# A second order for every step and load ahead of the experts, in an attention and mixture-of-experts kernel

## Chip, cores and metric

The kernel runs on one core of a Trainium2 chip. The metric is the device time of one execution in microseconds (us), lower is better. A core has the matrix engine (PE, with its weight loads shown as PEld), the vector engine (DVE), the scalar engine (ACT), GpSimd (POOL) and SP, which here issues all DMA transfers from one queue. [...]

## What is computed

Three blocks follow each other on 1152 tokens (2 batches of 576):

```
scores = q k^T / 8, masked: 4 heads to the last 32 positions, 4 heads to every 4th of the last 128
x  = softmax(scores) v                                # 8 heads of 64 -> 512 columns
h  = x w_in;  s = h softmax(h);  ln = (s - mean) / sqrt(var + 1e-6) * g      # 512 -> 1024
y  = ln w_out                                         # 1024 -> 512
out = sum over 4 experts of p_e relu(y w1_e) w2_e     # 512 -> 1024 -> 512
```

The matrices w_in and w_out come as 64-bit floats and are converted on the chip. Every large product is made of three: a value is split into a high part that the fast product takes exactly and a low part, and high x high, high x low and low x high are added up.

## The kernel before

The program is written out by hand, without a planner at run time: each engine executes its instructions in the order in which the program issues them, and semaphores make one engine wait for another. For everything up to the first half of expert 0 that order is a text, `ORDER`, of 542 entries. An entry is a load (a DMA from SP), a batch of warm-up products or the next step of a generator, and the loop that plays it is short:

```
for name in ORDER.split():
    name, _, n = name.partition("*")
    alt[0] = name.endswith("+")
    ...
        if name not in gens:
            gens[name] = makers[part[0]](*args)
        next(gens[name], None)
```

So the n-th time that `H.3` stands in the text, the n-th step of generator `H.3` is issued, and the text decides for each engine, and for SP's queue, what stands ahead of what. A sign `+` behind a name sets `alt`: in that step `pick()` gives POOL and not DVE, `copy` DVE and not ACT, `poolv` DVE and not POOL. The names:

- `F.n`: n warm-up products of constant data (L86). `lP`, `lD`: loads of a q/k tile (L151), by t and batch. `lvp`, `lvd`: of v (L159, L154). `lI.j`: of a quarter of w_in (L209, L212; `lI.4` and `lI.0` are the two halves of quarter 0). `lO`: of w_out (L228). `misc`: of small constants. `lW`, `lV`: of expert weights (L477).
- `UP.t.b`, `UD.t.b`: an attention unit, windowed or dilated heads: mask and scores (L266, L275), row maximum (L296), difference (L298), exponential (L301), sum (L303), reciprocal (L305), multiply (L307), transpose on PE (L326) and copy, or for five units of batch 1 a transpose on DVE (L312) that goes through DRAM (L316, L320), value product (L337), high part (L176 or L174) and low part (L250).
- `VI.j`, `VO.j.t`: conversion of a piece of w_in or w_out: two steps on ACT (L190, L192), two on DVE (L194, L196), an add (L198, `pick()`), the high part, the low part (L225, `pick()`; for w_out L241).
- `H.t`: the product of token tile t with w_in in four groups of six (L367), the maximum (L372), the exponential (L374), the weighted product (L376) and the scaling (L379 on ACT or L381 on DVE). The first group of `H.0` needs `UP.0.0` and quarter 0 of w_in.
- `T.t`: the transpose of tile t: tiles 0 to 2 on PE (L398), with a high and a low part; tiles 3 to 8 with a transpose on DVE (L412, L414), a write to DRAM (L419, L422), a read-back (L428, L431), the high part (L176 or L174) and the low part (L436, `pick()`).
- `X.c.d`: the product of three tiles with w_out (L449); `X.0` needs tiles 0 to 2, `X.1` 3 to 5, `X.2` 6 to 8. `endA`, `endE`, `endH`, `endX` give memory back; `sc` makes the row scales (L664 to L671).
- `WP`, `WV`, `XQ`: splits and sums of the expert weights and of y for a Strassen product (L481); `u.s`: its seven products for a half of the tokens (L562); `d.t`: the down product (L634).

PSUM has two rings of two tiles: `psa` for attention, the transposes of tiles 0 to 2 and half of the expert products, `psm` for warm-ups, `H`, `X` and the other half. A product waits until the tile before the last one in its ring has been read. Behind `ORDER` loops write out the other seven expert halves in a fixed order.

Of the kernel before, what the change touches and what calls it, by code (L numbers as in the profile page):

```python
# [28 lines left out]
ASWAP = ("UD.0.1", "UD.1.1", "UD.2.1", "UP.1.1", "UP.2.1")  # L29

ORDER = """
F.3 lP.0.0+ UP.0.0 lI.4 VI.4+ lD.0.0 VI.4 F.1 UP.0.0+ UP.0.0 lD.1.0+ VI.4 F.1 lP.1.0+ UD.0.0 UD.1.0 UP.0.0 VI.4 lI.0 UP.0.0+ VI.4 VI.0 lP.2.0 UD.0.0 UD.0.0+
UD.0.0+ UP.1.0 UP.0.0+ VI.4+ UP.0.0+ UD.1.0 UD.1.0+ UP.1.0 F.10 lD.2.0+ UP.2.0 UD.1.0+ VI.0 UD.0.0 VI.0+ VI.0 UP.1.0+ UD.1.0 UP.1.0+ VI.4+ lI.1+ UD.1.0+ VI.0+
UD.2.0+ UD.1.0+ lI.2+ F.3 UD.0.0 UD.0.0+ VI.0 UP.1.0+ UP.2.0 lvp.0.0+ VI.1+ VI.1+ UP.1.0+ UP.2.0+ VI.0 lvd.1.0+ F.1 UP.0.0 UD.2.0 UD.2.0 UP.2.0 UP.0.0 F.4
UD.1.0 UD.0.0 F.3 VI.1+ UD.1.0 VI.2+ UP.0.0 VI.2 UD.0.0 UP.2.0+ UP.1.0+ VI.1 UP.0.0 VI.1 VI.1 VI.2 UP.0.0+ lI.3 UD.1.0+ VI.2+ UP.1.0 lvp.1.0 UD.1.0 H.0+ lvd.0.0
UP.1.0 VI.3 UP.2.0+ UD.1.0+ UP.1.0 UD.2.0 UD.0.0+ VI.1 VI.3+ VI.2 VI.3 UP.1.0 UP.1.0 lD.1.1+ UD.0.0 lO.0.0+ H.0+ UD.1.1 VI.3 VI.2 UD.2.0+ lO.0.1 misc+ UD.1.1
H.1 UD.2.0 lD.0.1+ lvd.2.0+ UP.2.0+ UD.1.1+ UD.0.0 VO.0.1 VI.2+ lvp.0.1 lP.0.1 UD.2.0 lvd.2.1 H.1 VO.0.1+ UD.2.0 UD.2.0 UD.0.1 VI.3 VO.0.1+ UD.1.1 UP.0.1 UD.0.1
VI.3 lD.2.1 lvp.2.0+ lP.2.1 UD.1.1 UP.0.1 H.0 UD.0.1+ UD.0.1 UP.0.1+ UD.0.1+ UD.0.1+ UD.2.0 VO.0.1+ VI.3+ VO.0.0 UD.2.1 VO.0.0 lP.1.1+ VO.0.1+ H.0 lO.1.1+
VO.0.0 UD.2.1+ UD.2.0 UP.0.1+ UD.2.0 UD.0.1+ H.0+ H.1 H.0+ UD.0.1+ UD.0.1 UD.2.1 VO.0.0 H.1 H.0 UD.0.1+ UD.1.1 endE+ VO.0.0+ UD.2.1+ UP.2.0 UP.2.0 UD.1.1+
UP.2.1+ lvd.0.1+ VO.0.1+ lvd.1.1 UP.2.1+ UP.0.1 UD.2.1+ UP.2.0 UP.0.1 UP.2.0 VO.1.1+ VO.0.1+ VO.1.1 H.2 H.2+ H.1+ UP.2.1+ H.0+ UP.0.1+ UD.1.1+ VO.0.0+ UP.0.1  # L40
VO.1.1+ UP.2.0 VO.0.0+ H.1+ T.0 UP.2.1 UP.0.1 T.0+ UD.1.1 UD.2.1+ lO.1.0+ H.1+ T.0 UP.0.1 VO.1.1+ VO.1.1+ H.3+ UP.2.1 lO.2.1+ H.2+ T.0+ VO.1.0+ UP.0.1 UP.0.1+
VO.1.0 UD.1.1 VO.1.1+ UP.2.1+ UP.1.1+ UD.0.1 VO.1.0+ UP.1.1+ VO.1.0 H.2+ VO.1.0+ UP.1.1 UP.2.1+ UD.0.1+ UD.0.1+ H.3+ UD.2.1+ UD.1.1 H.2 H.1+ VO.1.0 UP.1.1+ T.1+
H.3+ lO.2.0+ UD.2.1+ H.2+ UD.1.1 H.3 UD.1.1 UD.2.1+ VO.2.1+ UP.1.1 VO.1.0+ H.4+ VO.2.0 VO.1.1 UP.2.1 VO.2.0 T.1+ T.2 T.1 H.3+ UP.1.1 UP.1.1+ VO.2.0+ H.4 H.5+
lvp.1.1+ UD.2.1+ H.5+ VO.2.1+ UP.2.1 H.4 T.2 VO.2.1+ VO.2.0+ VO.2.1+ lvp.2.1+ UP.2.1 VO.2.0+ lO.3.0 VO.2.1+ H.4 T.2 VO.2.1+ UP.1.1+ T.1+ T.2 lO.3.1 UP.2.1 H.3+
# [761 lines left out]
```

## Time and profile before

| | us |
|---|---|
| median of 3 runs | 530.11 (528.92 to 531.44) |
| the profiled execution | 528.32 |
| its span, first to last instruction | 526.5 |
| PE busy | 513.6 (98%) |
| DVE busy | 356.4 (68%) |
| ACT busy | 190.6 (36%) |
| POOL busy | 186.7 (35%) |

The profile is of one execution, and all times of rows are from the start of its span. Busy is an engine's time under instructions; the end of a matrix product is modelled, so a busy PE is not PE at its best. "Idle before" in brackets is the engine's idle time ahead of a row, with what ended it.

### The profile page before, as it was taken

The numbers are of one execution on the slowest core, as the hardware profiler recorded it, in microseconds if no ns is written. First come the engines' busy times: TensorE is split into PE (matmuls) and PEld (weight loads), VectorE is DVE, ScalarE is ACT, GpSimd is POOL, SyncE is SP. The second block draws the span as 40 slices with busy tenths as digits, with TensorE's granted clock in tenths as the row PEclk, the third lists the DMA queues.
The fourth block names the chain that finished last, engine by engine and source line by source line (L and its number), as shares of the span: only waits on it lengthen the run. The fifth ranks groups of instructions, "written<-read, shape, count | busy, mean of one in ns | idle before, by whom it ended". The sixth has DMA issues, their size and how long they took to land.

```text
span 526.5 us, 9419 instructions
## 1 busy us (share of the span) xinstructions
PE 513.6 (98%) x3971; PEld 457.9 (87%) x3971; DVE 356.4 (68%) x474; ACT 190.6 (36%) x294; POOL 186.7 (35%) x131
## 2 busy tenths in 40 slices
...
GB/s 321 409 319 149 146 202 78 143 159 200 1 225 95 1 1 50 111 1 1 159 1 1 8 153 0 2 153 7 2 0 161 1 0 81 0 1 1 1 81 100
DMA packets 24490, 46.44 MB, mean 88 GB/s; under 512 B 4480, under 2 KB 9088, under 8 KB 24064
## 3 DMA queue, kind: packets, MB, share of 16 engines
...
q14 instruction: 11, 0.09, 0.1%
...
## 4 chain that ended last, share of the span: by engine, by line
PE 90%; DMA 4%; DVE 2%; ACT 1%; issue 1%; SPq 1%; ACTq 0%
PE pa L634 19%; PE pm L634 18%; PE pm L562 17%; PE pa L562 17%; PE pm L367 9%; PE pm L449 6%; DMA draw<-in_moe_w_in_dram 2%; PE pa L337 1%; DMA dt<-st 1%; DMA et<-dt 1%; PE pa L275 1%; PE pa L398 1%; SPq L151 0%; DVE hl L436 0%; ACT eva L192 0%
## 5 line engine op out<-in xcount | busy, mean ns | idle before, releaser
L575 DVE SCALAR_TENSOR_TENSOR hl<-ct,hh 128x512 fp32r<-128x512 f32 (+1 forms) x64 | 64.1, 1018 | 32.4 <-ACT hh L573 32.4
L573 ACT ACTIVATE hh<-ct 128x512 fp32r<-128x512 f32 (+1 forms) x64 | 42.2, 682 | 50.8 <-DVE ct L605 21.3
L634 PE MATMUL pa<-wl,hh 128*128 128x512 f32 (+1 forms) x148 | 57.3, 387 | 0.0
L634 PE MATMUL pa<-wh,hh 128*128 128x512 f32 (+1 forms) x148 | 57.2, 387 | 0.0
L634 PE MATMUL pa<-wh,hl 128*128 128x512 f32 (+1 forms) x148 | 57.1, 386 | 0.0
L562 PE MATMUL pm<-xoh,hl 128*128 128x256 f32 (+1 forms) x192 | 56.8, 296 | 0.0
L562 PE MATMUL pa<-xoh,hl 128*128 128x256 f32 (+1 forms) x192 | 56.8, 296 | 0.0
L562 PE MATMUL pm<-xol,hh 128*128 128x256 f32 (+1 forms) x192 | 56.8, 296 | 0.0
L562 PE MATMUL pa<-xol,hh 128*128 128x256 f32 (+1 forms) x192 | 56.8, 296 | 0.0
L562 PE MATMUL pm<-xoh,hh 128*128 128x256 f32 (+1 forms) x192 | 56.8, 296 | 0.0
L562 PE MATMUL pa<-xoh,hh 128*128 128x256 f32 (+1 forms) x192 | 56.8, 296 | 0.0
L634 PE MATMUL pm<-wl,hh 128*128 128x512 f32 (+1 forms) x144 | 55.7, 387 | 0.0
L634 PE MATMUL pm<-wh,hh 128*128 128x512 f32 (+1 forms) x144 | 55.7, 387 | 0.0
L634 PE MATMUL pm<-wh,hl 128*128 128x512 f32 (+1 forms) x144 | 55.6, 386 | 0.0
L481 POOL TENSOR_TENSOR wl<-wl,wh 128x1024 fp32r<-128x1024 f32 x7 | 16.9, 2413 | 94.7 <-ACT wh L176 94.7
L639 DVE SCALAR_TENSOR_TENSOR xf<-pm,pr,xf 128x512 f32<-128x512 f32 (+1 forms) x32 | 23.6, 738 | 31.1 <-PE pm L634 31.1
L639 DVE SCALAR_TENSOR_TENSOR xf<-pa,pr,xf 128x512 f32<-128x512 f32 (+1 forms) x32 | 23.6, 738 | 30.3 <-PE pa L634 30.3
L589 POOL TENSOR_TENSOR ct<-ct,ct 128x512 f32<-128x512 f32 (+1 forms) x16 | 24.1, 1506 | 54.3 <-ACT ct L587 54.3
L176 ACT CAST wh<-wl 128x1024 fp32r<-128x1024 f32 x16 | 16.8, 1052 | 70.3 <-PE pa L634 39.8
L481 POOL TENSOR_TENSOR hl<-sw,hh 128x512 fp32r<-128x512 f32 x20 | 29.4, 1475 | 28.2 <-ACT hh L176 28.2
L562 PEld LDWEIGHTS pm<-xoh,hh 128*128 128x128 f32 x192 | 36.4, 190 | 0.3
L562 PEld LDWEIGHTS pm<-xol,hh 128*128 128x128 f32 x192 | 36.4, 190 | 0.3
...
## 6 DMA issues: line engine op xcount, KB each, us to landing
...
```

Source lines behind the costliest of these rows:

```text
L176: nc.scalar.copy(out, in_)
L275: nc.tensor.matmul(ps[32 * g:32 * g + 32, j, 64 * m:64 * m + 64], lhsT=qt[rows, h, xq:xq + 32], rhs=kt[rows, h, xq:xq + 64], start=False, ...
L337: nc.tensor.matmul(po[64 * (g % 2):64 * (g % 2) + 64, j, o:o + 32], lhsT=vt[rows, m, g, :], rhs=pt[rows, m, g, :], start=True, stop=True)
L367: nc.tensor.matmul(pm[:, n, :], lhsT=xx[:, kk, cols], rhs=ww["in", kk][:, 512 * n:512 * n + 512], start=(n_ == 0 and i < 2), stop=(n_ == K ...
L449: nc.tensor.matmul(pm[:, dd, 0:CW], lhsT=w_, rhs=x_[:, f, :], start=(f == 0 and i == 0), stop=(f == KF - 1 and i == 2))
L481: pick().tensor_tensor(out=out, in0=a, in1=b, op=op)
L562: nc.tensor.matmul(ps[:, ff, 0:n], lhsT=a[:, kk, fc], rhs=b[:, kk, :], start=kk == 0 and m == 0, stop=kk == 1 and m == 2)
L573: nc.scalar.activation(out=hv, in_=src, func=AF.Relu)
L575: nc.vector.scalar_tensor_tensor(out=lv, in0=src, scalar=0.0, in1=hv.bitcast(F32), op0=ALU.max, op1=ALU.subtract)
L589: poolv().tensor_tensor(out=c12, in0=c21, in1=c22, op=ALU.add)
L634: nc.tensor.matmul(po[:, 0, 0:dn], lhsT=h_[:, f, cols], rhs=w_, start=(f == 0 and i == 0), stop=(f == 3 and i == 2))
L639: nc.vector.scalar_tensor_tensor(out=acc[:, t, dc], in0=po[:, 0, 0:dn], scalar=pr[:, t, e:e + 1], in1=acc[:, t, dc], op0=ALU.mult, op1=ALU ...
```

## The change

The text `ORDER` is another arrangement of the same 542 entries; no entry is added or dropped, and the steps, tiles and instructions are the same. Since the sign stands at the entry, 51 steps change their engine with it. The lines of the text that matter below, from its start, from the stretch with the last tiles of batch 1, and from the end of the layer norm:

```
@@ ORDER = """ @@
-F.3 lP.0.0+ UP.0.0 lI.4 VI.4+ lD.0.0 VI.4 F.1 UP.0.0+ UP.0.0 lD.1.0+ VI.4 F.1 lP.1.0+ UD.0.0 UD.1.0 UP.0.0 VI.4 lI.0 UP.0.0+ VI.4 VI.0 lP.2.0 UD.0.0 UD.0.0+
-UD.0.0+ UP.1.0 UP.0.0+ VI.4+ UP.0.0+ UD.1.0 UD.1.0+ UP.1.0 F.10 lD.2.0+ UP.2.0 UD.1.0+ VI.0 UD.0.0 VI.0+ VI.0 UP.1.0+ UD.1.0 UP.1.0+ VI.4+ lI.1+ UD.1.0+ VI.0+
-UD.2.0+ UD.1.0+ lI.2+ F.3 UD.0.0 UD.0.0+ VI.0 UP.1.0+ UP.2.0 lvp.0.0+ VI.1+ VI.1+ UP.1.0+ UP.2.0+ VI.0 lvd.1.0+ F.1 UP.0.0 UD.2.0 UD.2.0 UP.2.0 UP.0.0 F.4
-UD.1.0 UD.0.0 F.3 VI.1+ UD.1.0 VI.2+ UP.0.0 VI.2 UD.0.0 UP.2.0+ UP.1.0+ VI.1 UP.0.0 VI.1 VI.1 VI.2 UP.0.0+ lI.3 UD.1.0+ VI.2+ UP.1.0 lvp.1.0 UD.1.0 H.0+ lvd.0.0
-UP.1.0 VI.3 UP.2.0+ UD.1.0+ UP.1.0 UD.2.0 UD.0.0+ VI.1 VI.3+ VI.2 VI.3 UP.1.0 UP.1.0 lD.1.1+ UD.0.0 lO.0.0+ H.0+ UD.1.1 VI.3 VI.2 UD.2.0+ lO.0.1 misc+ UD.1.1
-H.1 UD.2.0 lD.0.1+ lvd.2.0+ UP.2.0+ UD.1.1+ UD.0.0 VO.0.1 VI.2+ lvp.0.1 lP.0.1 UD.2.0 lvd.2.1 H.1 VO.0.1+ UD.2.0 UD.2.0 UD.0.1 VI.3 VO.0.1+ UD.1.1 UP.0.1 UD.0.1
-VI.3 lD.2.1 lvp.2.0+ lP.2.1 UD.1.1 UP.0.1 H.0 UD.0.1+ UD.0.1 UP.0.1+ UD.0.1+ UD.0.1+ UD.2.0 VO.0.1+ VI.3+ VO.0.0 UD.2.1 VO.0.0 lP.1.1+ VO.0.1+ H.0 lO.1.1+
-VO.0.0 UD.2.1+ UD.2.0 UP.0.1+ UD.2.0 UD.0.1+ H.0+ H.1 H.0+ UD.0.1+ UD.0.1 UD.2.1 VO.0.0 H.1 H.0 UD.0.1+ UD.1.1 endE+ VO.0.0+ UD.2.1+ UP.2.0 UP.2.0 UD.1.1+
...
-VO.1.1+ UP.2.0 VO.0.0+ H.1+ T.0 UP.2.1 UP.0.1 T.0+ UD.1.1 UD.2.1+ lO.1.0+ H.1+ T.0 UP.0.1 VO.1.1+ VO.1.1+ H.3+ UP.2.1 lO.2.1+ H.2+ T.0+ VO.1.0+ UP.0.1 UP.0.1+
-VO.1.0 UD.1.1 VO.1.1+ UP.2.1+ UP.1.1+ UD.0.1 VO.1.0+ UP.1.1+ VO.1.0 H.2+ VO.1.0+ UP.1.1 UP.2.1+ UD.0.1+ UD.0.1+ H.3+ UD.2.1+ UD.1.1 H.2 H.1+ VO.1.0 UP.1.1+ T.1+
...
-VO.2.0+ H.5+ UP.1.1+ VO.3.0 UP.2.1+ VO.2.0 H.5+ VO.2.1+ UP.2.1+ UP.1.1+ H.5+ VO.3.1 VO.3.0+ UD.2.1+ VO.3.1 VO.3.0 UD.2.1 X.0.1+ X.0.0 VO.3.1+ UP.1.1+ VO.3.0+
-VO.3.1 VO.3.0+ VO.3.0 VO.3.1 endA T.3+ VO.3.1 VO.3.1 T.3+ UP.1.1 VO.3.0+ H.4+ T.3+ X.0.1+ T.4 X.0.0+ H.5 X.0.0 UP.1.1 T.4+ X.0.1+ T.4 T.3+ T.5+ UD.2.1 H.6+ T.3
-H.8 T.3+ T.5+ H.6+ T.5 H.6 H.6+ T.4+ H.6 T.5+ H.7+ T.6 T.4 H.8 H.8 T.5 T.4 H.8+ T.5+ H.8+ H.7 X.1.0 T.6 T.6 T.6 T.8+ H.7 T.8+ H.7 T.6+ T.8+ T.6 H.7+ T.8+ X.1.0+
-T.7+ T.8+ X.1.1 X.1.1+ T.7+ T.8 T.7+ sc T.7 endH T.7+ T.7 X.1.0 XQ.0 X.1.1 X.2.0 XQ.0 XQ.0 lW.0 WP.0+ WP.0 X.2.1+ XQ.0 WP.0 WP.0 WP.0 XQ.0 XQ.0 XQ.0+ WP.0 u.0+
...
+lI.4 lP.0.0+ F.1 lD.1.0+ F.1 F.10 VI.4+ lD.0.0 VI.4 VI.4 UP.0.0 F.4 VI.4 UP.0.0+ VI.4+ UD.1.0 UP.0.0 lI.0 lP.1.0+ UP.0.0 UP.0.0+ F.3 lD.2.0+ UD.1.0 lP.2.0 lI.1+
+VI.4 lI.2+ UP.0.0+ VI.0 VI.0 UD.0.0 UD.1.0+ UD.0.0 lvp.0.0+ UD.1.0+ UD.0.0+ UP.1.0 VI.0+ UD.1.0 UP.0.0+ VI.0 VI.0+ F.3 lvd.0.0 UD.1.0+ lvd.1.0+ UD.0.0+ UD.0.0
+UD.0.0 lI.3 UP.1.0 misc+ UD.0.0+ UD.2.0+ UP.1.0+ UD.2.0 lD.1.1+ F.1 UD.2.0 VI.0 lvp.1.0 UD.1.0+ lD.0.1+ UP.2.0 VI.4+ UP.1.0+ UD.2.0 VI.1+ UP.1.0+ lvd.0.1+
+UP.1.0+ UD.2.0+ VI.1+ VI.0+ UP.2.0 UP.2.0+ UP.0.0 UD.1.0 lvd.2.0+ VI.1+ lP.0.1 VI.1 UD.2.0 F.3 UP.0.0 UD.1.0 VI.2+ VI.1 lO.0.1 VI.2 UD.0.0 VI.2 UP.0.0 UD.0.0
+UD.1.0+ UP.0.0 VI.1 UP.0.0+ UP.1.0+ UD.1.0 UD.0.0+ lO.0.0+ UD.0.0 VI.2+ VI.2+ UD.1.0+ UP.2.0 lD.2.1 lP.1.1+ UD.0.0 H.0+ UP.1.0 UP.2.0+ UP.1.0 UP.2.0+ VI.1
+UP.2.0+ UD.1.1 UP.1.0 VI.2 VI.3 H.0+ UD.1.1 VI.2 UP.1.0 VI.3+ UD.1.1+ H.0 UD.2.0+ UD.2.0 UP.1.0 lvd.1.1 UD.0.1 VI.3 VI.3 UD.1.1 lP.2.1 UD.2.0 UD.0.1 UP.0.1
+lvp.2.0+ UP.0.1 UD.0.1+ UP.0.1+ H.1 VO.0.1 VO.0.1+ UD.0.1 VI.3+ H.1 VI.3 UD.1.1 UD.0.1+ VO.0.1+ UD.2.0 UD.2.1 UD.0.1+ VO.0.1+ VI.3 UD.2.0 UD.2.1+ VO.0.0 UD.2.0
+H.0 H.0+ UD.1.1 VO.0.1+ VO.0.0 VO.0.0 H.1 UD.0.1+ H.1 UD.0.1+ UP.0.1+ endE+ H.0+ UP.2.0 UD.2.1 UP.2.0 VO.0.1+ VO.0.0 UP.2.1+ lvp.0.1 lO.1.1+ UP.2.0 H.0 H.1+
...
+VO.1.0+ UP.2.0 H.1+ H.2+ UP.0.1 T.0 VO.1.0 UP.0.1 VO.0.1+ UD.1.1 lvd.2.1 UP.0.1 T.0+ H.3+ UP.2.1 VO.1.0+ H.2+ VO.1.0 T.0 T.0+ UP.0.1 UP.0.1+ UD.2.1 UD.1.1
+UP.2.1+ VO.1.0+ H.2+ UP.2.1+ UD.0.1 UD.0.1 H.2 UD.0.1+ UP.1.1+ lO.2.0+ VO.1.1 VO.1.1+ UP.1.1+ VO.1.0 H.1+ VO.1.0+ UP.1.1 VO.1.1+ H.2+ VO.1.1+ VO.2.0 H.3+
+UD.2.1+ VO.2.0 UD.1.1 UP.1.1+ UD.2.1+ T.2 UD.1.1 H.3+ VO.2.0+ VO.2.0+ H.3 UD.1.1 VO.1.1+ T.2 lO.2.1+ H.4+ UP.2.1 VO.2.0+ UP.1.1 T.2 H.3+ UP.1.1 T.1+ VO.1.1
...
+T.1+ VO.2.1+ H.4 UP.2.1 X.0.1+ H.5+ UP.2.1 lvp.1.1+ UP.2.1+ UP.1.1+ UD.2.1+ UP.1.1+ VO.3.0 H.5+ VO.3.0+ VO.2.1+ endA T.3+ H.5+ VO.3.1 VO.3.0 H.4+ VO.3.0+ VO.3.0
...
+H.6+ H.6+ H.8 T.3 T.5+ H.6 H.6+ T.4+ H.6 T.5 T.4 T.3+ T.6 T.5+ H.8 T.5 T.6 T.5 T.4+ H.8 H.8+ H.7+ H.8 T.8+ X.1.1 H.7 T.6 H.7 T.6 T.8+ H.7 X.1.0 X.1.1+ X.1.0+
+H.7 T.7+ T.6 T.7+ T.8+ T.6 T.7+ T.8+ T.7 endH lW.0 sc T.8+ T.8 WP.0+ X.1.1 T.7+ WP.0 X.1.0 T.7 WP.0 XQ.0 WP.0+ XQ.0+ WP.0 X.2.0 WP.0 WP.0 WP.0 XQ.0 XQ.0 WP.0
...
```

## Rows read from the trace of the kernel before

**Rows 1.** Table by stretch: start:end, length, busy us (instructions) of PE, PEld, DVE, ACT, POOL, granted clock, DMA share, GB/s.
```profile
0.00:46.80 46.80, 39.20 (x931) 26.69 (x931) 40.87 (x85) 27.67 (x44) 17.69 (x26) 1.00 0.82 311
46.80:111.40 64.60, 64.60 (x633) 56.15 (x630) 52.26 (x82) 42.97 (x68) 14.86 (x12) 1.00 0.49 152
111.40:131.00 19.60, 17.56 (x99) 16.65 (x98) 11.68 (x19) 8.20 (x14) 2.81 (x2) 1.00 0.60 181
131.00:181.00 50.00, 50.00 (x312) 48.06 (x313) 48.16 (x59) 18.17 (x28) 22.93 (x14) 1.00 0.25 85
181.00:526.50 345.50, 342.25 (x2005) 310.37 (x2003) 203.46 (x232) 93.61 (x143) 128.40 (x80) 1.00 0.12 41
```

**Rows 2.** Chain of work that ended last, 117 to 129 us: start, us, what.
```profile
117.34 0.57 SPq L431
...
118.62 5.57 DMA dt<-st
...
124.86 4.09 DMA et<-dt
```

**Rows 3.** Timeline of PE to 58 us: start, us, engine, line, operation, shapes, count.
```profile
1.44 1.46 PE L86 MATMUL pm<-warm 128*128 128x512 bf16 x3 [1.44 <-DVE warm L81]
...
3.97 0.97 PE L275 MATMUL pa<-qkP 64*32 64x64 f32 x48
...
13.95 0.72 PE L275 MATMUL pa<-qkP 64*32 64x64 f32 x48
...
24.41 0.70 PE L367 MATMUL pm<-wh,xhi 128*128 128x512 f32 x2
...
57.34 0.34 PE L266 MATMUL pa<-mask,identb 128*128 128x192 bf16 x2
```

**Rows 4.** Timeline of DVE, 4 to 131 us.
```profile
4.98 0.56 DVE L296 TENSOR_REDUCE st<-pa 128x6 f32<-128x384 f32 x1 [0.55 <-PE pa L275]
...
6.39 0.43 DVE L194 TENSOR_SCALAR cva<-cva 128x512 uint32<-128x512 uint32 x1 [0.26 <-ACT cva L192]
6.85 0.69 DVE L196 SCALAR_TENSOR_TENSOR cva<-draw,cva 128x512 uint32<-128x512 uint32 x1
...
7.93 0.68 DVE L198 CUSTOM_DVE_ANT_0 cva<-draw,cva 128x1024 uint16<-128x1024 uint16 x1
...
44.85 1.21 DVE L376 SCALAR_TENSOR_TENSOR e<-e,pm 128x1024 f32<-128x1024 f32 x1
...
55.90 1.23 DVE L250 TENSOR_TENSOR hl<-pa,hh 128x1024 fp32r<-128x1024 f32 x1 [0.71 <-ACT hh L176]
...
82.72 1.68 DVE L198 CUSTOM_DVE_ANT_0 cva<-cvr,cva 128x1024 uint16<-128x1024 uint16 x1
...
117.23 1.24 DVE L414 STREAM_TRANSPOSE st<-e 128x1024 f32<-128x1024 f32 x1
```

**Rows 5.** Timeline of POOL, 4 to 131 us.
```profile
14.20 1.30 POOL L198 TENSOR_TENSOR cva<-cva,draw 128x512 uint32<-128x512 uint32 x1 [2.22 <-DVE cva L196]
...
82.21 1.64 POOL L198 TENSOR_TENSOR cva<-cva,cvr 128x512 uint32<-128x512 uint32 x1 [7.48 <-DVE cva L196]
...
110.00 2.39 POOL L436 TENSOR_TENSOR hl<-et,hh 128x1024 fp32r<-128x1024 f32 x1 [9.38 <-ACT hh L176]
```

**Rows 6.** DMA issues of the whole span: count, KB each, median us to landing.
```profile
vd<-in_vd_dram SPq DMA_DIRECT2D x6, 384.0 KB, 8.5
```

**Rows 7.** Timeline of PE, 111 to 132 us, with its idle time in brackets.
```profile
112.44 0.44 PE L449 MATMUL pm<-hl,wh 128*128 128x384 f32 x1 [0.65 <-POOL hl L436]
...
129.77 0.41 PE L449 MATMUL pm<-hh,wh 128*128 128x384 f32 x1 [0.59 <-issue]
130.99 0.45 PE L449 MATMUL pm<-hl,wh 128*128 128x384 f32 x1 [0.80 <-DVE hl L436]
```

**Rows 8.** Timeline of SP's DMA issues, 94 to 131 us.
```profile
106.60 0.36 SPq L422 DMA_DIRECT2D dt<-st  x1
109.44 1.24 SPq L431 DMA_DIRECT2D et<-dt  x2
```

More of the change, by code (lines that the diff above doesn't have):

```diff
@@ L40 @@
-UP.2.1+ lvd.0.1+ VO.0.1+ lvd.1.1 UP.2.1+ UP.0.1 UD.2.1+ UP.2.0 UP.0.1 UP.2.0 VO.1.1+ VO.0.1+ VO.1.1 H.2 H.2+ H.1+ UP.2.1+ H.0+ UP.0.1+ UD.1.1+ VO.0.0+ UP.0.1
-VO.1.1+ UP.2.0 VO.0.0+ H.1+ T.0 UP.2.1 UP.0.1 T.0+ UD.1.1 UD.2.1+ lO.1.0+ H.1+ T.0 UP.0.1 VO.1.1+ VO.1.1+ H.3+ UP.2.1 lO.2.1+ H.2+ T.0+ VO.1.0+ UP.0.1 UP.0.1+
-VO.1.0 UD.1.1 VO.1.1+ UP.2.1+ UP.1.1+ UD.0.1 VO.1.0+ UP.1.1+ VO.1.0 H.2+ VO.1.0+ UP.1.1 UP.2.1+ UD.0.1+ UD.0.1+ H.3+ UD.2.1+ UD.1.1 H.2 H.1+ VO.1.0 UP.1.1+ T.1+
-H.3+ lO.2.0+ UD.2.1+ H.2+ UD.1.1 H.3 UD.1.1 UD.2.1+ VO.2.1+ UP.1.1 VO.1.0+ H.4+ VO.2.0 VO.1.1 UP.2.1 VO.2.0 T.1+ T.2 T.1 H.3+ UP.1.1 UP.1.1+ VO.2.0+ H.4 H.5+
```

12 lines of the change are left out of this document (7 added, 5 removed).

## The prediction

> **What bounds the kernel now.** I read the page first: PE, the matrix engine, is busy nearly all of the span. That sum hides where the slack is, so the next view is the table by stretch [rows 1]. From 181 us on, PE is busy 342.25 of 345.50 us, and from 131 to 181 us all 50.00. The order under change ends at about 181 us, when the last product of the first expert half is issued; behind it the program is written out by loops that the diff doesn't touch. In 46.8 to 111.4 PE is full as well (64.60 of 64.60). So PE has idle time that an order can win back in two places: 46.80 - 39.20 = 7.6 us ahead of 46.8 us, and 19.60 - 17.56 = 2.04 us between 111.4 and 131. Part of PE's busy time in the first stretch is warm-up products too, which compute nothing and fill waits.
>
> The two places have different limits. In the first, DVE (VectorE) is busy 40.87 of 46.80 us and DMA 0.82 of its share at 311 GB/s [rows 1]: PE waits for conversions and softmax steps there. In the second, DVE has 11.68 of 19.60 us, and the chain of waits runs through DRAM transfers [rows 2]: tile 7 of the layer norm is written to DRAM and read back transposed, and the first products that take it stand until its low half is there.
>
> **What the change moves.** It removes and adds no instruction. Of the 542 entries nearly all change place, and 51 steps change engine by the sign behind their name: 16 go from DVE to POOL (GpSimd), 14 from POOL to DVE, 14 from DVE to ACT (ScalarE), 7 from ACT to DVE. PE's own list hardly differs: from the second token tile on its entries are the same but for a few swapped neighbours. Four pieces matter.
>
> *One, the start.* The first transfer becomes the first half-row of w_in and not the first q/k tile, and twelve warm-up products stand ahead of the first scores instead of three. Three warm-ups took 1.46 us at the slow clock [rows 3], so twelve take 12 x 1.46/3 = 5.8 us and PE comes to the first scores at 1.44 + 5.8 = 7.2 us less what a faster clock gives back. Before they began at 3.97. [...] Here PE runs without a pause from its first product. If the faster level came at once, at half the pitch, the twelve would take 2.9 us and the scores start 0.4 us late; if never, 3.2. I take 2.5, nearer to never, since it had not come by 3.97 before. The q/k tile itself, now behind 512 KB of w_in, lands up to 0.524 MB / 311 GB/s = 1.7 us later [rows 1], at 5.7 or before: the warm-ups hide it. Everything of unit UP.0.0 hangs on these scores, and on it the first expert-input product, at 24.41 [rows 3]. Against that, w_in's first half-row comes first, so that its two DVE steps (0.43 + 0.69 = 1.12 us [rows 4]) run while DVE would wait for scores; before they stood between UP.0.0's steps. That leaves 2.5 - 1.1 = +1.4 us.
>
> *Two, DVE's load up to token tile 1.* Up to the weighted product of tile 0 (L376), DVE runs 66 instructions of the list before, from 4.98 to 44.85 [rows 4]; after the change 63 stand ahead of it, because the adds of VI.4, VI.2 and VI.3, a subtraction, a cast and a multiply go to POOL and ACT while the subtractions of VI.2 and VI.3 come back. By the durations of the same steps this is 41.2 against 39.1 us: -2.1 us where DVE sets the time. POOL was busy 17.69 of 46.80 us [rows 1] and has the room. But an add that took DVE 0.68 us takes POOL 1.30 [rows 4, 5], so each conversion that moves gets longer while DVE gets free. Bounds for pieces one and two together: -2.1 (DVE sets the time all through, and the start is absorbed) and +2.5 (the late scores come through and nothing is regained). I take +1.4 and half of the relief: 1.4 - 1.05 = +0.35 us.
>
> Of the loads: vd.0.0 goes ahead of the last quarter of w_in, so this one lands 384 KB later, 0.393 MB / 311 GB/s = 1.3 us [rows 1, 6]; its conversion is used by the fourth group of tile 0's products, in the list twelve PE steps behind the first, which cover it. vp.1.0 is moved behind two more loads; its user moves back too. The w_out loads go behind five others, with their first cast moved as well. All three are counted at nothing; without cover the first costs 1.3 us, which lies inside the bound. vp.1.1 is now the last of its kind, right ahead of the reads of the swapped UP.1.1; late, it would hold one product of that unit, a microsecond at most, and that is left to the range.
>
> *Three, the ring of two PSUM tiles.* The value product of UD.0.1 now stands ahead of UP.1.1's scores. It takes the buffer that tile 0's transposes hold until the low-half subtraction at 55.90 (1.23 us) is done [rows 4]; before, UP.1.1 took it. DVE was done at 57.13 and these scores started at 57.34 [rows 3], so there was little to spare. Between 0 and one such subtraction, 1.23, I take +0.3, nearer to 0, because fewer DVE instructions stand ahead of it (80 against 84).
>
> *Four, the end of the layer norm.* PE stood three times in this stretch: 0.65 us for POOL's low half of tile 5, 0.59 and 0.80 us for tile 7 [rows 7], in sum the 2.04 of the table. The first is POOL's 2.39 us at 110.00 [rows 5]; the step goes to DVE, and tile 4's, which is ready earlier, goes to POOL. For tile 7 the SP queue is what changes. Before, T.8's read-back was issued at 117.34 and T.7's write at 118.62, behind it; the write took 5.57 us [rows 2]. T.6's write, with no read-back ahead, was issued at 106.60 and its reader went at 109.44, so 2.84 [rows 8]. In the new list T.7's write is ahead of T.8's read-back, which saves 5.57 - 2.84 = 2.7 us on the chain; T.7's own read-back then queues behind T.8's, which may take back part. The chain needs to be 0.59 + 0.80 = 1.4 us shorter for PE not to stand. T.7's transpose (117.23 [rows 4]) comes no later: the two DVE steps of T.6 that stood ahead of it are one on ACT and one behind. Bounds: -2.04 and 0. I take -1.8, nearly all, since 2.7 is twice what is needed.
>
> Behind 131 us both lists have the same products in nearly the same places and PE never stood; the down products move behind the next up products, which gives their inputs more time. Counted at nothing, with DVE's 48.16 of 50.00 us [rows 1] as what could turn this.
>
> **The sum:** 0.35 + 0.3 - 1.8 = -1.15 us. The profiled execution took 528.32 us (span 526.5 and 1.8 around it) and would take 527.2; it lies 1.8 under the median of the three runs, 530.11, which would become 529.0. A measurement of this kernel tells about 0.5%, 2.65 us, from no change.
>
> [...] DVE's add at 82.72 took 1.68 us where the same add took 0.68 at 7.93 [rows 4]; POOL ran an add from 82.21 to 83.85 [rows 5], and DVE's ended 0.55 after that: it stood until POOL was done. [...] By it, work given to POOL can cost DVE time as well; that is rival three.
>
> **Rivals.**
> 1. *DVE's relief comes through whole.* For it: 40.87 of 46.80 us. Against: PE's first input is later. -2.1 + 0 - 2.04 = -4.1: 526.0.
> 2. *Slower: the late start comes through.* Place: the score chain of UP.0.0, decisive once the first expert-input product starts over 2 us after 24.41. Then the start costs 2.5 and the ring 1.23, less 1.8: +1.9: 532.0. For it: PE's list gives no other work early. Against: DVE could do conversions meanwhile.
> 3. *POOL holds DVE.* VI.4's add (1.30) and those of VI.2 and VI.3, twice as wide (an estimate, 2 x 1.30 each): 6.5 us on POOL. If DVE stood for all of it, less the about 3.1 us that these adds took DVE (0.68 and, by width, 2 x 1.2), +3.4, with the ring at 0.3 and -1.8: +1.9: 532.0. [...]
> 4. *The layer norm's gain doesn't come:* T.7's read-back waits for T.8's as long as the write did. 0.35 + 0.3 = +0.65: 530.8.
>
> **Chances.** Forecast 0.45 (527.5 to 530.5), rival 1 0.28 (524.5 to 527.5), rival 2 0.09, rival 3 0.05, rival 4 0.13. Under 527.46 lies nearly all of rival 1 and a tail of the forecast: 0.33. Over 532.76 lie somewhat under half of rivals 2 and 3, a little of 4, and what I have not thought of: 0.12. Within: 0.55. The range that leaves out 2 in 10 is 524.8 to 532.6.
>
> **What would show it.** Right: PE's first scores at 6 to 7 us; the first expert-input product at 24 to 26 us; T.7's write landing within 3.5 us; PE without idle between the last expert-input product and the experts; the same 345 us from the last product of the order to the end. Wrong: that product under 23 us or over 27; a wait on PE for tile 7 of over 1 us; PE idle in the stretch that was full; a PE wait for conversions behind the start of the experts.

## The result, and the profile after

The changed kernel takes 533.15 us (median of 20 runs, 530.74 to 535.59) where the kernel before takes 529.26 (20 runs, 528.10 to 531.44). The ratio is 1.0072, with a 95% interval of 1.006 to 1.0085: some 3.9 us slower. The forecast was 529.0, a gain of 1.15 us. The profiled execution of the changed kernel took 533.49 us, with a span of 531.7 against 526.5.

The table by stretch of the changed kernel, in the columns of [rows 1]; its steps stand some microseconds later, so the same stretch holds a little less of the program:

```profile
0.00:46.80 46.80, 38.29 (x827) 26.74 (x828) 35.99 (x75) 26.46 (x41) 20.59 (x27) 0.89 0.83 313
46.80:111.40 64.60, 62.81 (x707) 54.83 (x706) 49.35 (x83) 42.73 (x71) 12.51 (x10) 0.97 0.47 141
111.40:131.00 19.60, 19.27 (x103) 17.89 (x102) 13.77 (x22) 7.63 (x13) 4.23 (x2) 1.00 0.47 145
131.00:181.00 50.00, 49.42 (x310) 47.33 (x309) 41.78 (x51) 21.98 (x34) 24.37 (x15) 1.00 0.34 112
...
20.00:25.00 5.00, 4.05 (x146) 3.32 (x144) 4.47 (x6) 4.56 (x7) 0.00 (x0) 0.75 1.04 407
25.00:30.00 5.00, 2.59 (x7) 2.10 (x8) 2.19 (x5) 1.21 (x3) 2.38 (x1) 0.59 1.03 395
30.00:35.00 5.00, 5.00 (x110) 3.90 (x109) 3.79 (x7) 3.58 (x5) 2.40 (x2) 0.73 1.02 400
87.00:91.00 4.00, 3.93 (x14) 3.93 (x15) 3.90 (x8) 2.16 (x3) 0.00 (x0) 0.57 0.51 166
```

In the row of the layer norm's end PE is busy 19.27 of 19.60 us, but since every step is 5 to 6 us later there, the wait for tile 7 now lies in the next row (0.6 us at 135.75). The stretch that had been full, 46.8 to 111.4, now has 1.79 us without work, and in 25 to 30 us every engine stands for about half of the time or more (PE busy 2.59 of 5.00 us) at a DMA share of 1.03. The records of the granted clock hold two values, 1.00 and 0.50, below called the faster and the lower level. The kernel before has 1.00 throughout, in records that begin at 12.02 us; the changed kernel, with records from 5.41 us on, has 0.50 from 19.06 to 22.47, 25.89 to 32.72 and 87.33 to 90.74 us. PE stood from 16.66 to 18.49, 24.86 to 27.41 and 85.28 to 87.07.

Four places on PE divide the loss. "Before" and "after" are the starts of the same product in both traces:

| first product of | before | after | later by | added in the stretch |
|---|---|---|---|---|
| H.2 | 46.77 | 49.43 | 2.66 | +2.66, the opening |
| H.6 | 95.10 | 101.24 | 6.14 | +3.48, a wait at X.0 |
| u.0 | 147.57 | 152.35 | 4.78 | -1.36, the end of the layer norm |
| end of the span | 526.54 | 531.70 | 5.16 | +0.38, the experts |

**The opening.** PE's timeline of the changed kernel, the rows that answer to [rows 3]:

```profile
1.44 4.70 PE L86 MATMUL pm<-warm 128*128 128x512 bf16 x12 [1.44 <-DVE warm L81]
...
6.24 0.72 PE L275 MATMUL pa<-qkP 64*32 64x64 f32 x48
...
12.42 0.25 PE L266 MATMUL pa<-mask,identb 128*128 128x192 bf16 x1
13.84 0.24 PE L266 MATMUL pa<-mask,identb 128*128 128x192 bf16 x1 [1.18 <-issue]
...
23.00 1.87 PE L337 MATMUL pa<-pt,vd 64*64 64x32 f32 x94 [0.64 <-ACT pt L176]
27.41 0.42 PE L337 MATMUL pa<-pt,vd 64*64 64x32 f32 x2 [2.55 <-issue]
27.76 1.22 PE L367 MATMUL pm<-wh,xhi 128*128 128x512 f32 x2
```

The scores begin at 6.24, as forecast. The loss is the row at 27.41. UD.0.0's value product stops after 46 of its 48 products, with all its data there, and waits 2.55 us for "issue", which is nothing that the profile names. The first expert-input product stands behind it and begins at 27.76 instead of 24.41. What came in that pause is in the list of DMA queues for 24.8 to 26 us (queue, kind: packets, MB, share of 16 engines):

```profile
q1 hardware_dynamic: 153, 0.46, 98.9%
q8 instruction: 1, 0.02, 5.6%
```

One packet of instructions, among loads that take 98.9% of the engines' time. In the packed records of both traces q8 brings 31 such blocks of 16 KB (16,384 bytes) in the run, and the one of this pause is moved from 24.86 to 25.94 us; PE goes on 1.47 us later. Counted in PE's records (weight loads, products and semaphore instructions) the stop stands after the 961st. The shorter stop of the changed kernel, ahead of 13.84, stands after record 449, 512 earlier. The kernel before has stops of the same kind inside value products:

```profile
26.90 0.36 PE L337 MATMUL pa<-pt,vp 64*64 64x32 f32 x10 [0.15 <-issue]
...
38.97 0.67 PE L337 MATMUL pa<-pt,vd 64*64 64x32 f32 x31 [0.87 <-issue]
```

They stand after the same record 961 and after record 1,473, 512 later. By this count PE stood at the end of a block of its instructions until the next one had come (it went on 1.24 to 1.47 us after the block's end at these four stops). The blocks count as 256 records: 31 of them come in a run of 7,989 records, 258 for one, and c2 below stops halfway between 961 and 1,473 too.

The opening thus turns on which side of record 961 a step stands. Ahead of the first product of H.0 the trace of the kernel before has 877 records, that of the changed kernel 966. PE comes to record 706, the first of the block ahead, at 21.16 us before and 21.20 after; the next one lands at 25.45 before and 25.94 after, and PE goes on at 26.90 and 27.41. Before, the first six products of H.0 ran ahead of that point; after, they stand behind it.

**The wait at X.0.** DVE's timeline of the changed kernel, 81 to 87 us:

```profile
81.75 0.20 DVE L656 TENSOR_TENSOR pr<-gp_sb,pr_s 128x36 f32<-128x36 f32 x1
84.65 1.25 DVE L414 STREAM_TRANSPOSE st<-e 128x1024 f32<-128x1024 f32 x1 [2.70 <-PE pa L337]
85.82 1.18 DVE L376 SCALAR_TENSOR_TENSOR e<-e,pm 128x1024 f32<-128x1024 f32 x1
```

and PE's in the same stretch:

```profile
83.68 0.90 PE L337 MATMUL pa<-pt,vd 64*64 64x32 f32 x48
84.40 0.88 PE L337 MATMUL pa<-pt,vp 64*64 64x32 f32 x48
87.07 0.49 PE L449 MATMUL pm<-hh,wh 128*128 128x384 f32 x1 [1.79 <-DVE e L376]
```

T.3's transpose (L414) kept DVE idle 2.70 us, waiting for UD.2.1's value product, which the new order puts behind the first half of X.0.1 on PE. (By the code, the transpose writes into memory that `endA` takes back from the attention tiles.) H.5's product with the exponentials (L376) stands behind that transpose on DVE, though ACT was done with the exponentials at 81.56:

```profile
81.37 0.19 ACT L374 ACTIVATION_READ_ACCUMULATOR e<-pm,nmx 128x1 f32 x1
```

L376 frees the PSUM tile (`pm`) that X.0.0 takes. So X.0.0 begins at 87.07 after 1.79 us, and its next products come every 0.32 us instead of 0.175; the granted clock reads 0.57 in 87 to 91 us, against 1.00 before.

**The end of the layer norm.** From the chain of work that ended last, against [rows 2]:

```profile
124.23 4.64 DMA dt<-st
...
128.88 0.57 SPq L431
...
129.50 4.22 DMA et<-dt
```

T.7's write took 4.64 us where it had taken 5.57. SP's timeline shows T.8's read-back issued 1.1 us behind it, so that both were on their way together; that this made the write longer was not tested.

```profile
124.23 0.37 SPq L422 DMA_DIRECT2D dt<-st  x1
125.34 4.78 SPq L431 DMA_DIRECT2D et<-dt  x4
```

From PE's waits of 111 to 180 us (in total, times, longest):

```profile
PE pm L449 <- DVE hl L436: 0.6, 1, 0.6
PE pm L449 <- DVE e L376: 0.3, 1, 0.3
```

The first is the wait for tile 7, at 135.75; the second, at 122.28, is new.

### The profile page after: what moved, and what is told of

It is laid out like the page before. It is cut to its first block, busy times and chain, and to the rows that moved or that the text cites. A ratio compares the mean times of both kernels' runs of the same rounds, so it can differ in the third digit from the quotient of the medians.

```text
span 531.7 us, 9418 instructions
## 1 busy us (share of the span) xinstructions
PE 517.2 (97%) x3971; PEld 461.8 (87%) x3971; DVE 348.7 (66%) x465; ACT 194.0 (36%) x301; POOL 189.4 (36%) x133
## 4 chain that ended last, share of the span: by engine, by line
PE 90%; DVE 4%; DMA 3%; issue 1%; ACT 0%; SPq 0%; DVEq 0%; ACTq 0%
PE pa L634 19%; PE pm L634 18%; PE pm L562 17%; PE pa L562 17%; PE pm L367 8%; PE pm L449 7%; PE pa L337 2%; DMA et<-dt 2%; DMA dt<-st 1%; PE pm L86 1%; PE pa L275 1%; DVE e L376 1%; DVE sm L298 1%; DVE st L296 1%; PE pa L326 1%
## 5 line engine op out<-in xcount | busy, mean ns | idle before, releaser
L562 PEld LDWEIGHTS pa<-xoh,hh 128*128 128x128 f32 x192 | 36.4, 190 | 0.7 <-DVE ct L593 0.4
## 6 DMA issues: line engine op xcount, KB each, us to landing
draw<-in_moe_w_in_dram SPq DMA_DIRECT2D x3, 1024.0 KB, 12.9
```

Of the source, the lines that this page charges most:

```text
L562: nc.tensor.matmul(ps[:, ff, 0:n], lhsT=a[:, kk, fc], rhs=b[:, kk, :], start=kk == 0 and m == 0, stop=kk == 1 and m == 2)
```

## The experiments

Each run is compared with runs of the kernel before on the same chip; those medians lie between 528.5 and 529.8 us. Ratios are to the kernel before, with their 95% intervals.

### Is it the count of instructions? a1 and b1

a1 takes ten warm-up products from the changed kernel:

```diff
-... UP.0.0+ F.3 lD.2.0+ ... VI.0+ F.3 lvd.0.0 ... lD.1.1+ F.1 UD.2.0 ... UD.2.0 F.3 UP.0.0 ...
+... UP.0.0+ lD.2.0+ ... VI.0+ lvd.0.0 ... lD.1.1+ UD.2.0 ... UD.2.0 UP.0.0 ...
```

> The changed kernel without ten of its 26 warm-up products (three behind UD.1.0's scores, three behind UP.1.0's, one behind UD.2.0's, three behind UD.1.0's transpose): 20 records fewer on TensorE ahead of H.0, no other step moved. The trace of the changed kernel has TensorE stop at 24.64 after 961 records in the middle of a value product whose data are all there, and go on at 27.41, 1.5 us after a block of its own instructions landed; the kernel before stops after 1,473 records, 512 later. Theory one (instructions): the stop belongs to the count of records, not to a step. Then the first expert-input product of H.0, 20 records nearer, falls ahead of the stop: it begins at 24.8 to 25.3 instead of 27.76, the stop moves behind it into UP.1.0's transposes, still ending at about 27.4; H.2 begins at 46.8 to 47.8 instead of 49.43 and the time is 530.2 to 531.5. Theory two (a load that lands late): the product waits for data, and begins at 27.4 to 28.0; the time is 533.1, within 0.7. Theory three (the late scores themselves): as two, or worse for the lower clock that fewer warm-ups leave, 533 to 535.

b1 adds 48 narrow products to the kernel before; their result is unused:

```diff
-... UP.0.0 VI.2 UD.0.0 ...
+... UP.0.0 N.48 VI.2 UD.0.0 ...   # N: 48 products, 64x64 by 64x32, on the warm-up tile
```

> The kernel before with 48 narrow products (64x64 by 64x32, on the warm-up tile, result unused) behind UP.0.0's value product, where TensorE waits 1.22 us for a copy: 96 records more, some 0.8 us of work, no other step moved. Theory one (instructions): the first product of H.0 falls behind the 961st record, and so begins when the next block of instructions has landed, at 26.7 to 27.3 instead of 24.41; H.2 begins at 47.8 to 49.5 instead of 46.77, the time is 530.3 to 532. Theories two and three (a load, the late scores): nothing of that is changed here; the first product begins at 24.4 to 25.0, and the time is 529.3 to 529.9.

Measured: a1 530.32 us, ratio 1.0035 (1.002 to 1.005); b1 531.37 us, ratio 1.0053 (1.0032 to 1.0075). PE's timelines, first a1, then b1:

```profile
23.32 2.78 PE L337 MATMUL pa<-pt,vd 64*64 64x32 f32 x96 [0.64 <-ACT pt L176]
26.03 1.22 PE L367 MATMUL pm<-wh,xhi 128*128 128x512 f32 x2
```

```profile
23.23 0.89 PE L337 MATMUL pa<-pt,vd 64*64 64x32 f32 x44
26.80 0.30 PE L337 MATMUL pa<-pt,vd 64*64 64x32 f32 x2 [2.68 <-issue]
27.03 0.59 PE L326 MATMUL pa<-ident,pd 128*128 128x128 f32 x3
27.33 1.15 PE L367 MATMUL pm<-wh,xhi 128*128 128x512 f32 x2
```

In a1 the stop is gone, the value products run through, and H.2 begins at 47.67 instead of 49.43. The first expert-input product came at 26.03, not at 25: with fewer warm-ups the granted clock was 0.50 in 20 to 25 us and 0.55 in 25 to 30, where the changed kernel has 0.75 and 0.59. So it also came to record 962 at 28.97, 2.7 us after that block had landed (26.26), and the stop did not move behind that product, as expected, but went. In b1 the kernel before got the stop and the late product, and nothing was added but 96 records and their 0.8 us of work, in a wait. H.2 came at 52.12, outside the expected range: b1 has another stop of 1.20 us ahead of 44.11, after record 1,729, again a multiple of 256 behind 961. Its time lies in the range. The row of the table from 0 to just ahead of the restart shows the same place; first the changed kernel, then b1, then a2 (below):

```profile
0.00:27.30 27.30, 18.90 (x477) 11.43 (x477) 20.33 (x49) 14.87 (x23) 12.55 (x22) 0.91 0.94 355
```

```profile
0.00:26.70 26.70, 18.84 (x474) 11.64 (x477) 21.02 (x50) 13.28 (x20) 8.89 (x20) 1.00 0.95 363
```

```profile
0.00:29.40 29.40, 18.18 (x472) 11.35 (x477) 20.46 (x49) 14.92 (x23) 12.90 (x22) 0.91 0.95 362
```

The first two numbers in brackets count PE's products and its weight loads: 477 weight loads had been made in all three when PE stopped. (A few product records are missing from the traces.) Theory one stands; a late load would not keep count.

### Do the loads make the blocks late? e1

> The kernel before with eight copies of 512 KB from DRAM to DRAM (results unused) issued on SP behind vd.1.1 at about 49 us, where the DMA engines are mostly free: nothing but transfers is added. [...] The time itself says little, since the copies also stand ahead of other transfers.

```diff
-... lvd.1.1 UP.2.1+ ...
+... lvd.1.1 Z.8 UP.2.1+ ...   # Z: 8 copies of 512 KB, DRAM to DRAM, results unused
```

Measured: in the kernel before, PE comes to the first record of a block at 53.93 us, and the next block begins 0.77 us later, at a DMA share of 0.46 in 54 to 59 us. In e1, PE entered that block at 54.2 us, and the next one began at 58.09, 3.9 us later, at a share of 1.04. The list of DMA queues of e1 for 58 to 59 us:

```profile
q1 hardware_dynamic: 157, 0.29, 99.4%
q8 instruction: 1, 0.02, 7.1%
```

So with full DMA engines a block was late at this place too, where it was not late before; it is one block of one run. In both traces the first four blocks begin 3.2 to 3.9 us after PE enters the one ahead, and the ones from 45 to 65 us 0.4 to 1.1 us after it. What starts a block is not shown: behind 115 us, among long products, most blocks begin 1 to 5 us ahead of that entry, so that the lags compare like with like only at the same place, as e1 does. The one run took 543.4 us, which says nothing here: PE stood 12.9 us (for DVE's L250, by the profile), with loads queued behind the copies.

### The late scores alone: b3

```diff
-F.3 lP.0.0+ UP.0.0 ... UP.1.0 F.10 lD.2.0+ ...
+F.12 lP.0.0+ UP.0.0 ... UP.1.0 F.1 lD.2.0+ ...
```

> The kernel before with twelve warm-up products ahead of the first scores instead of three, and one behind UP.1.0's scores instead of ten: the same records, no other step moved. Theory one (the late scores cost nothing by themselves, the count of records does): scores at 6 to 7 us, but the first product of H.0 at 24.2 to 25.0, H.2 at 46.5 to 47.3, the time within 0.6 of the kernel before. Rival (the late scores come through): H.0 at 26.5 to 27, the time 1.8 to 2.6 above. The prediction's own term for the late scores was +0.35, with bounds of -2.1 and +2.5.

Measured: 528.75 us, ratio 0.9996 (0.998 to 1.0012). The scores began at 6.98, the first expert-input product at 26.01, later than theory one had it, and H.2 at 47.28, 0.5 us late. In the time nothing of it shows. The late scores come through to the first product but not, within this interval, to the time.

### The wait at X.0: a2

```diff
-... endA T.3+ H.5+ VO.3.1 ...
+... endA H.5+ T.3+ VO.3.1 ...
```

> The changed kernel with one step moved on VectorE: T.3's transpose stands behind H.5's product with the exponentials (L376) instead of ahead of it. Theory one (order on VectorE): T.3's transpose waits for UD.2.1's value product at 83.68, which stands behind half of X.0.1, and holds H.5's L376, which frees the PSUM bank of X.0.0. With the swap X.0.0 begins at about 85.3 instead of 87.07, the granted clock stays 1.00 through 80 to 96, H.6 begins at 97.6 to 98.2 instead of 101.24, and the time is 529.5 to 530.2. Theory two (UP.1.1's value product and its load vp.1.1, moved back in the queue, make the wait): X.0.0 still begins at about 87, the time is 533.1 within 0.5. Theory three (the pause alone goes, the lower clock comes all the same): 531.2 to 531.7.

Measured: 530.20 us, ratio 1.0033 (1.0018 to 1.0048). Its trace has no wait on PE from 80 to 96 us, and the granted clock there is 1.00. From H.3 (59.02) to H.6 (99.69) it took 40.67 us where the changed kernel took 44.10 (57.14 to 101.24): 3.43 less, the step that theory one expected (3.0 to 3.6), though H.6 itself came 1.5 us later than it said. The gain in the median, 0.0039 of the time or 2.1 us, is less. In the profiled run the stop in the opening was longer, 3.84 us with the block beginning at 26.88 instead of 24.86; how much that varies from run to run was not measured.

### H.0 ahead, with T.3 behind: a3

```diff
-... UD.0.0+ lO.0.0+ UD.0.0 VI.2+ VI.2+ UD.1.0+ UP.2.0 lD.2.1 lP.1.1+ UD.0.0 H.0+ UP.1.0 ...
+... lO.0.0+ VI.2+ VI.2+ UD.1.0+ H.0+ UD.0.0+ UD.0.0 UP.2.0 lD.2.1 lP.1.1+ UD.0.0 UP.1.0 ...
```

and the edit of a2.

> The changed kernel with both moved: H.0's first six products stand ahead of UD.0.0's value product on TensorE, as in the kernel before, and T.3's transpose behind H.5's L376. If both causes are as theories one have it, H.0 begins at 25.0 to 25.4, UD.0.0's value product takes the stop, H.2 begins at 46.7 to 47.7, H.6 at 95 to 96, and the time is 526.5 to 527.8, below the kernel before: the end of the layer norm keeps its 1.4 us. If the start's loss was a load's, H.0 begins at 27.4 or later and the time is 529.5 to 530.2.

Measured: 531.69 us, ratio 1.0046 (1.0029 to 1.0064). That was a miss. The table by stretch of a3:

```profile
20.00:25.00 5.00, 4.35 (x101) 3.69 (x100) 4.75 (x6) 4.17 (x7) 0.00 (x0) 0.50 1.03 404
25.00:30.00 5.00, 4.60 (x57) 3.32 (x56) 1.23 (x4) 1.56 (x5) 2.41 (x1) 0.50 1.03 396
30.00:35.00 5.00, 4.37 (x102) 3.54 (x102) 4.97 (x8) 3.86 (x7) 3.38 (x2) 0.50 1.02 399
```

H.0 began at 24.41, and no stop came; but the granted clock was 0.50 for all of 20 to 35 us, and H.2 began at 50.85. In 25 to 30 us DVE has 1.23 of 5 us: its work comes out of UD.0.0's value product, which now stands behind six long products that took 2.86 us at 0.50, against 1.57 at 1.00 before. The trace bears this out as far as it goes: ACT stood 3.44 us for that product ahead of 28.84, and DVE 3.36 us for ACT ahead of 29.71. It was not tested by itself.

### The price of the lower clock: d1

```diff
-... UP.1.0 F.10 lD.2.0+ ... lI.2+ F.3 UD.0.0 ... lvd.1.0+ F.1 UP.0.0 ... UP.0.0 F.4 UD.1.0 UD.0.0 F.3 VI.1+ ...
+... UP.1.0 lD.2.0+ ... lI.2+ UD.0.0 ... lvd.1.0+ UP.0.0 ... UP.0.0 UD.1.0 UD.0.0 VI.1+ ...
```

> The kernel before without its 21 warm-up products behind the fifth: 42 records fewer, so no stop ahead of H.0 can come of the count; what is left is the granted clock. If the clock has a price of its own in the opening, it is 0.5 in most of 12 to 30, H.0 begins at 24.4 to 26.5, H.2 at 47.5 to 49.5 and the ratio is 1.001 to 1.005. If only the stop costs, H.2 begins at 45.8 to 46.9 and the ratio is at most 1.000.

Measured: 528.99 us, ratio 1.0002 (0.999 to 1.0014). The clock column reads 1.00, but the six first products took 2.84 us (25.11 to 27.95) where they had taken 1.57; in a3, at a recorded 0.50, they took 2.86 (24.41 to 27.27), so I take PE to have been at the lower level. H.2 began at 47.25, 0.5 us later than before and between the two expected ranges. But 42 records fewer also took away the two stops of the kernel before (0.15 and 0.87 us): its trace has none behind 14 us. The lower level and the missing stops together cost nothing that this measurement shows; the price of the level alone stays open.

### Which part of the list? b2, x1, x2 and c3

b2 is the list of before up to H.6's first entry and the new order behind it; x1 is the same with the cut at H.2; x2 is x1 with the edit of a2; c3 is x2 with two entries of VO.1.0 behind the copy of UP.0.1:

```diff
-... VO.1.0+ UP.2.0 H.1+ H.2+ UP.0.1 T.0 VO.1.0 UP.0.1 UD.1.1 ...   # x2; the last UP.0.1 here is the copy
+... UP.2.0 H.1+ H.2+ UP.0.1 T.0 UP.0.1 VO.1.0+ VO.1.0 UD.1.1 ...   # c3
```

> The kernel before up to the first step of H.6, and from there the order of the changed kernel: the end of the layer norm, the preparation of the first expert and what follows, alone. Theory one (the end of the layer norm gives back what it gave in the changed kernel): from the end of H.7's product to u.0 the changed kernel took 34.6 us and the kernel before 36.0, so u.0 begins 1.4 us earlier, at about 146.2 instead of 147.57, some 0.4 of it is lost in the u and d block, and the time is 527.3 to 528.0 where the kernel before has 528.5 (ratio 0.998 to 0.999). Theory two (that gain is only the clock's or the later start's, made where the loads and VectorE were already behind): u.0 begins at 147.3 to 148, the ratio is 1.000 to 1.002.

> The kernel before up to the first step of H.2 (its opening, its loads, its warm-ups), and from there the order of the changed kernel. If the opening's loss is all made ahead of H.2, H.2 begins at 46.6 to 47.2 and H.3 at 54.3 to 55; then the wait of X.0.0 behind T.3's transpose comes as in the changed kernel (1.8 us, with a lower clock behind it 3.4), and the end of the layer norm gives 1.4 back: the time is 1.8 to 2.6 above the kernel before (ratio 1.0035 to 1.005). If the wait of X.0.0 needs the late opening (a step that is late because everything was), it does not come, and the ratio is 0.997 to 0.999.

> As x1_open_before, with T.3's transpose behind H.5's L376 besides. Both losses are then undone and the end of the layer norm stays: H.6 begins at 94.9 to 95.6, u.0 at 145.9 to 146.6, and the time is 0.6 to 1.4 below the kernel before (ratio 0.9975 to 0.999). Against it: if the changed order between H.2 and X.0 has a loss of its own that the two others hid, it shows here as H.6 later than 96, and the ratio is above 1.

> As x2_open_before_t3, with the two conversions of VO.1.0 on ScalarE behind the copy of UP.0.1's transposed probabilities instead of ahead of it: in the two mixed orders they waited for a load (2.6 us) and held that copy, and TensorE with it (2.8 us at 53.5). Without it H.3 begins at 54.2 to 55 instead of 57.9, H.6 at 95 to 96, and the ratio falls from 1.0052 to 0.997 to 0.9995, the end of the layer norm being the only difference left. If some other wait comes in its place, H.3 begins at 56 or later and the ratio stays above 1.002.

Measured: b2 528.64 us, ratio 0.9991 (0.9977 to 1.0006); x1 534.29 us, 1.0095 (1.0067 to 1.0123); x2 532.52 us, 1.0052 (1.0032 to 1.0071); c3 530.46 us, 1.0023 (1.0008 to 1.0039).

In b2 u.0 began at 147.93 and not at 146.2: X.1's first products waited 1.9 us for L376 of the softmax ahead of them, so the gain at the end of the layer norm is not to be had with this cut. x1 missed high because the mixed list makes a wait of its own at 53.5 us; its PE timeline:

```profile
52.44 1.04 PE L398 MATMUL pa<-ident,e 128*128 128x128 f32 x8
56.11 1.48 PE L337 MATMUL pa<-pt,vp 64*64 64x32 f32 x48 [2.64 <-ACT pt L176]
```

What x1 does show is the wait at X.0: 1.8 us for L376 again, with an opening that is not late. x2 takes it away, and the ratio falls by 0.0043. c3 takes the wait at 53.5 away, and another (2.1 us for a low half, L250, behind H.3's first products) comes in its place, so the mixed lists never came to compare the middles cleanly.

### Both causes undone: c1 and c2

c1 is a1 and a2 together. c2 drops all warm-ups but the first twelve, adds five behind UP.0.0's transposes, and has the edit of a2:

```diff
-... UP.2.0+ UP.0.0 UD.1.0 lvd.2.0+ ...
+... UP.2.0+ UP.0.0 F.5 UD.1.0 lvd.2.0+ ...   # and without the other fourteen
```

> The changed kernel with both undone as they stood alone: ten warm-up products fewer, and T.3's transpose behind H.5's L376. If the two losses are separate, the gains add: 1.0072 less 0.0037 for the stop and less 0.0039 for the wait of X.0.0 is a ratio of 0.9996 to the kernel before, 0.998 to 1.0015; H.6 begins at 95.3 to 96.2. If they share a cause (everything after H.2 only follows the opening), the ratio stays at 1.002 or more.

> The changed kernel with T.3's transpose behind H.5's L376, without fourteen warm-up products (all but the twelve ahead of the first scores) and with five new ones behind UP.0.0's transposes, where TensorE waits 2.0 us: nine products, 18 records, fewer in all. If the granted clock of the opening falls because TensorE waits there at 16 to 19 us, it stays at 1.00 through 20 to 25, H.0 begins at 24.6 to 25.2 and H.2 at 45.8 to 46.9, and the ratio is 0.9965 to 0.999. If the lower clock comes from later waits, H.2 begins at 47.4 to 48 as with ten warm-ups fewer, and the ratio is that of the run beside it, 0.998 to 1.0015.

Measured: c1 527.69 us where the kernel before has 528.97, ratio 0.9974 (0.9961 to 0.9987); c2 527.94 us, 0.9986 (0.9969 to 1.0002). The gains add, to somewhat more than their sum, and c1 is faster than both kernels. Its H.6 began at 95.78 and u.0 at 147.11, 51.33 us apart against 52.47 before: the end of the layer norm kept 1.1 us.

c2 kept the clock: 1.00 in 20 to 35 us, H.0 at 24.70. And H.2 began at 48.08, outside the expected 45.8 to 46.9 and later than at a clock of 0.50 in c1 (47.40). The rows of its table from 0 to just ahead of four restarts of PE:

```profile
0.00:14.50 14.50, 8.85 (x223) 4.54 (x224) 9.90 (x32) 5.57 (x9) 5.37 (x16) 1.00 0.87 319
0.00:27.90 27.90, 18.57 (x475) 11.37 (x477) 22.36 (x53) 15.81 (x25) 13.27 (x23) 0.94 0.94 358
0.00:34.00 34.00, 24.39 (x602) 16.02 (x604) 27.24 (x59) 20.59 (x33) 15.52 (x24) 0.95 0.96 366
0.00:40.20 40.20, 29.49 (x730) 19.89 (x731) 32.73 (x69) 23.22 (x36) 18.63 (x26) 0.96 0.92 353
```

PE stops at 224, 477, 604 and 731 weight loads; the second is the place of the stop in the changed kernel, the last that of the kernel before ahead of 38.97. The profile puts the pauses ahead of 34.20 and 40.40 down to "issue", the one ahead of 28.09 to POOL, though it ends 1.36 us after a block did (26.73). The blocks that came in these three pauses began 1.0 to 1.1 us later than the same ones in c1. At a clock of 1.00 PE got its instructions no sooner here than at 0.50.

## Why the prediction was wrong

**The start (piece one) was right in what it priced.** Twelve warm-ups, scores at 6 to 7 us, the faster level within them: 6.24 us, the warm-ups 0.40 to 0.43 us apart up to 5.25 and 0.22 from 5.55 on, and 48 scores in 0.72 us. The 2.5 us that was taken for the lateness, a choice between 0.4 and 3.2, no run shows; the scores came 2.27 us later (3.97 to 6.24). b3 prices the lateness at nothing in the time. Rival two's sign came true, a first product over 2 us after 24.41, and its 532.0, which rival three shares, lies nearest to 533.15; its mechanism, the score chain, did not. Two of the prediction's own signs of being wrong came: this product behind 27 us (27.76), and PE idle in the stretch that had been full.

**Two steps failed. The first is the bound of the opening.** The prediction took PE there to wait for data alone, from DVE or a load, and so put the start and DVE's relief together as +0.35 with bounds of -2.1 and +2.5. It measured +2.66. PE was held by its own instructions: the new order has three value products of 96 records each, the third being UD.0.0's, ahead of H.0, where before two stood, so 966 records stand ahead of H.0 and not 877, and it fell just behind record 961. No duration of a step shows this; the count of records ahead of a step does. The stop and what came with it (0.50 from 25.89 to 32.72 us) came to 2.0 us in the time by a1.

**DVE's relief (piece two)** came and bought nothing that shows. The 63 instructions up to tile 0's L376 take 38.8 us in the trace of the changed kernel (39.1 was forecast), against 41.2 for the 66 before; and with the stop gone H.2 was still 0.6 to 0.9 us later than before (c1, a1), at the lower clock of these runs (0.50 in 20 to 25 us, 0.50 and 0.55 in 25 to 30). Rival three, POOL holding DVE, does not show: DVE's steps are as long as before (L196 on 1,024 columns 1.22 us in both).

**The loads, counted at nothing,** were not the cause: the 2.55 us stand under "issue". In a2's trace, with the same opening, value products waited 0.54 and 1.03 us for vp and vd, ahead of a stop that ended 1.5 us after its block landed; how much of the wait came through is not known.

**The second step that failed is the stretch from tile 2 to tile 6, priced at nothing** beside piece three, but for a microsecond in the range for vp.1.1; PE's only wait there is the one for L376. It measured +3.48. The prediction said that PE's list behind the second tile differs by a few swapped neighbours, and followed across engines only the one of piece three. Two swaps did it together: UD.2.1's value product behind half of X.0.1 on PE, and T.3's transpose ahead of H.5's L376 on DVE. In the trace they cost 1.79 us of standing and 1.7 more, with a clock of 0.57 in 87 to 91 us; in the time, by a2, 2.1 us. x1 shows that they do so without the late opening.

**The ring (piece three),** +0.3: from H.2 to H.4 the changed kernel takes 17.03 us (49.43 to 66.46) and the kernel before 16.99. It cost nothing.

**The end of the layer norm (piece four),** -1.8 with bounds of -2.04 and 0: the mechanism held, the size was -1.36 in the changed kernel and -1.1 in c1. T.7's write took 4.64 us and not under 3.5, so PE still waited 0.6 us for tile 7, under the 1 us that would have refuted it, and 0.3 us more for an L376. It is not a part that can be carried over alone (b2).

**Behind 131 us,** counted at nothing: +0.38 us.

**What stays open:** why the two gains, each measured alone, sum to a little less than c1 shows (a1 0.0037 and a2 0.0039 make 0.0076; c1, measured on another chip, lies 0.0098 below the changed kernel), which their intervals allow; how far the stop varies between runs, which could also explain the wide spread of the changed kernel; what the lower clock costs in the opening; and the loss in a3.
